# One of eight row maxima of a two-round step computed from a key-difference score, with PSUM banks and matmul order rearranged

## The chip, the cores and the metric

The kernel runs on one core of one Trainium2 chip. That core has a matrix engine (TensorE, "PE" in the profile, with its weight loads shown as "PEld"), three engines for elementwise work (VectorE "DVE", ScalarE "ACT", GpSimd "POOL") and a queue engine (SyncE "SP") that issues most DMAs. Each engine works through its own list of instructions in order and waits on semaphores for the others. Matrix products land in PSUM, which here is used as eight banks of 128 x 512 float32 each. The metric is device time in microseconds, lower is better.

## The reference

Two complete multi-head attentions (A and B) read the same input `x` of 2048 tokens x 512, each with its own `wqkv` and `wo`, 32 heads of width 16, and a per-token gate mixes their results:

```python
def mha(x, wqkv, wo):                      # S = 2048, D = 512, H = 32, Dh = 16
    q, k, v = split_heads(x @ wqkv)
    scores = einsum("bhqd,bhkd->bhqk", q, k) * Dh ** -0.5
    return merge_heads(softmax(scores) @ v) @ wo

g = sigmoid((x * gate_w).sum(-1))
out = g * mha(A_x, A_wqkv, A_wo) + (1 - g) * mha(A_x, B_wqkv, B_wo)
```

Everything is float32. The softmax needs, for each of 64 heads and 2048 queries, the maximum of 2048 scores before the exponentials, so every score is formed twice: once with queries on the partitions for the maximum, and once with keys on the partitions for the exponential and the product with the values.

## The kernel before

**Prologue.** Queries, keys and values of all heads are projected on TensorE (`project_qk`, `project_v`), split into a high and a low float32r part, and written to DRAM (`qd`, `kd`, `vd`). From there `load_stacks` brings the two operands of one head into SBUF as `q_st` and `k_st`: 48 rows (high, low and high parts of 16 features) at partitions 0 and the same again at partition 64. Two matmuls that use different halves run beside each other in the array; `rows()` hands the halves out in turn. While the last projections run, `run_ahead` already forms the maxima of the first 20 query tiles (16 of head 0, four of head 1).

**Main loop.** A round is one head and one tile of 128 keys; there are 64 x 16 = 1024 rounds, and the loop takes two at a time (`for r in range(0, ROUNDS, 2)`); these two rounds together are called a *step* below, and eight steps are a *head*. In a step TensorE does, in the order that the string `FULL` writes out:

- `e`, eight times: one score matmul (50 rows, 128 keys x 512 queries; the two extra rows subtract the maximum) into a bank of `ps_st`, whose exponential ScalarE writes to `p` (`score`).
- `m` and `M`, three parts for each of two query tiles that lie 20 tiles ahead (`max_part`): score matmuls of 128 queries x 512 keys. An `m` forms one block of 512 keys into a bank of `ps_m1` (two banks); an `M` forms two blocks into the double bank of `ps_m2`. VectorE reduces each part to its maximum, one column of `mxp`. That is four reductions over 512 and two over 1024 per step: the eight blocks of two query tiles.
- a digit: so many quarters (128 queries each) of the product of `p` with the values (`attend`), four blocks of keys side by side in the array, accumulated in the bank `acc`. A quarter's `p` was made in the step before. Before the first digit of a step the due output projections (`project_out`, 12 or 9 matmuls) are placed, in 32 steps of the run.

`tc.manual_schedule()` makes the order of the program the order on each engine. PSUM holds two banks `ps_m1`, two (one double) `ps_m2`, three `ps_st` and one `acc`; a tile of a pool takes its pool's banks in turn, and a matmul into a bank waits until the bank's previous content has been read.

**At the end of a head's maxima** (every 16 query tiles, in the steps where r mod 16 is 10), `max_split` reduces `mxp` to one value per query on VectorE (`mrow`, L135), GpSimd splits that in two (`mparts`, L136 and L137), and in the next step `max_rows` transposes it on VectorE (`mt`, L142) and sends it through DRAM into the two extra rows of `q_st`. The step with r mod 16 = 12 begins the next head's maxima. When a head's last `attend` is done (r mod 16 = 0), ScalarE copies `acc` to SBUF (`ev`, L549), and the next head's first product waits for that.

GpSimd's other work is placed by `at(round, ...)`: the gate's products (L313, L320), the value loads (L158), normalization and splitting of finished outputs (L389, L394, L395). These calls are emitted at the head of their step, ahead of the step's matmuls.

## Time and profile before

| what | value |
| --- | --- |
| median of 3 runs | 2851.66 us (2851.09 to 2851.94) |
| span of the profiled execution, first to last instruction | 2848.8 us |
| PE busy | 2830.3 us (99%) |
| DVE busy | 2559.5 us (90%) |
| ACT busy | 2260.3 us (79%) |
| POOL busy | 225.3 us (8%) |
| main loop, first exponential to the last head's maxima | about 294.6 to 2775 us |

The profiled execution's own time is its span, 2848.8 us; the runs shown have 2.9 us more. Matmuls are pipelined and their ends are modelled, so a PE that is busy 99% of the time is not for that reason at its peak. In the main loop's share of the span DVE is busy nearly all the time as well. A row of the timeline has the start in us, the length in us, the engine, the line, the operation, output and inputs, the shapes, a count where several followed each other, and in brackets the idle time before it with what ended it.

### The profile page before, as it was taken

The page shows a single profiled execution, that of the slowest core. Times are in us where ns is not written, and L with a number is a line of the kernel's source. Part 1 is how long each engine was busy: PE and PEld are TensorE (multiplying, and loading weights), DVE is VectorE, ACT ScalarE, POOL GpSimd, SP SyncE. Part 2 cuts the span into 40 slices and gives each one's busy share as a digit, 9 for nine tenths or more (in the row PEclk, how much of TensorE's full clock was granted, in tenths as well). Part 3 has the DMA queues.
Part 4 walks back from the last instruction along what each step waited for, and adds up shares of the span by engine and source line. Part 5 has one row for each costly group of instructions (what it writes and reads, how often), then busy time and mean ns, then how long its engine had stood idle before and what let it go on. Part 6 is the DMA issues. An engine that isn't in the chain of part 4 may idle for free.

```text
span 2848.8 us, 62282 instructions
## 1 busy us (share of the span) xinstructions
PE 2830.3 (99%) x26016; PEld 1372.6 (48%) x26016; DVE 2559.5 (90%) x3371; ACT 2260.3 (79%) x4253; POOL 225.3 (8%) x369
## 2 busy tenths in 40 slices
PE   8999999999999999999999999999999999999999
PEld 7877444444444444444444455444444444444544
DVE  4135899999999999999999988999999999998894
ACT  3221788889888888988988866888888888987775
POOL 1000232000000000000100231000000000011201
PEclk9999999999999999999999999999999999999999
DMA  7673333222332222332322342232222233323302
GB/s 244 195 230 121 88 80 80 40 49 54 66 58 55 52 56 46 54 56 55 85 55 49 95 101 55 54 56 48 59 47 55 55 74 66 54 67 85 72 10 91
DMA packets 83759, 214.65 MB, mean 75 GB/s; under 512 B 21878, under 2 KB 32086, under 8 KB 70934
## 3 DMA queue, kind: packets, MB, share of 16 engines
q1 hardware_dynamic: 80918, 201.76, 31.1%
q0 software_dynamic: 2560, 8.91, 1.2%
q8 instruction: 205, 3.36, 0.5%
q14 instruction: 76, 0.62, 0.1%
HBM read 145.87 MB, written 64.74 MB: 74 GB/s over the span
## 4 chain that ended last, share of the span: by engine, by line
PE 91%; DVE 7%; DMA 1%; ACT 0%; SPq 0%; issue 0%; POOL 0%; DVEq 0%; ACTq 0%
PE acc L532 34%; PE ps_st L583 29%; PE ps_m L123 14%; DVE mxp L125 7%; PE ps_pro L206 6%; PE ps_m L416 3%; PE ps_pro L229 3%; DMA raw<-in_xT 0%; DMA rb<-rd 0%; PE ps_st L416 0%; DVE rn L371 0%; PE ps_st L467 0%; ACT p L585 0%; PE ps_m L583 0%; PE ps_m L467 0%
## 5 line engine op out<-in xcount | busy, mean ns | idle before, releaser
L125 DVE TENSOR_REDUCE mxp<-ps_m 128x1 f32<-128x512 f32 (+1 forms) x3072 | 2419.6, 861 | 49.8 <-PE ps_m L123 43.5
L585 ACT ACTIVATE p<-ps_st 128x512 f32<-128x512 f32 x4056 | 2157.0, 601 | 332.6 <-PE ps_st L583 233.7
L583 PE MATMUL ps_st<-q_st,k_st 50*128 50x512 f32 x4056 | 1322.9, 445 | 0.0
L123 PE MATMUL ps_m<-k_st,q_st 48*128 48x512 f32 x4096 | 1199.0, 434 | 3.6 <-DVE mxp L125 3.1
L532 PE MATMUL acc<-p,vg 128*17 128x384 f32 (+1 forms) x16208 | 1188.3, 386 | 3.0 <-DVE ev L540 2.0
L583 PEld LDWEIGHTS ps_st<-q_st,k_st 50*128 50x128 f32 x4056 | 591.8, 184 | 745.7 <-ACT p L585 723.8
L123 PEld LDWEIGHTS ps_m<-k_st,q_st 48*128 48x128 f32 x4096 | 543.1, 185 | 105.6 <-DVE mxp L125 39.4
L532 PEld LDWEIGHTS acc<-p,vg 128*17 128x17 f32 x16208 | 314.0, 96 | 512.1 <-issue 481.0
L136 POOL CAST mparts<-mrow 128x16 fp32r<-128x16 f32 x64 | 12.5, 196 | 2194.5 <-DVE mrow L135 2194.5
L211 DVE TENSOR_TENSOR part<-ps_pro,part 128x1024 fp32r<-128x1024 f32 x32 | 39.2, 1225 | 110.5 <-ACT part L210 110.5
L210 ACT CAST part<-ps_pro 128x1024 fp32r<-128x1024 f32 x32 | 32.5, 1015 | 132.0 <-PE ps_pro L206 132.0
L416 PE MATMUL ps_m<-wo,ot 128*128 128x512 f32 (+1 forms) x354 | 90.4, 400 | 0.0
L206 PE MATMUL ps_pro<-xh,whi 128*128 128x512 f32 x256 | 73.2, 405 | 8.0 <-ACT xh L192 7.5
L232 ACT COPY v_st<-ps_pro 128x512 f32<-128x512 f32 x31 | 18.2, 587 | 77.4 <-PE ps_pro L229 77.4
L416 PEld LDWEIGHTS ps_m<-wo,ot 128*128 128x128 f32 (+1 forms) x354 | 64.0, 188 | 23.8 <-DVE mxp L125 8.7
L206 PE MATMUL ps_pro<-xh,wlo 128*128 128x512 f32 x256 | 69.3, 393 | 0.0
L206 PE MATMUL ps_pro<-xl,whi 128*128 128x512 f32 x256 | 69.2, 393 | 0.0
L206 PEld LDWEIGHTS ps_pro<-xh,whi 128*128 128x128 f32 x256 | 47.9, 192 | 23.1 <-ACT xh L192 10.2
L206 PEld LDWEIGHTS ps_pro<-xh,wlo 128*128 128x128 f32 x256 | 48.6, 190 | 10.3
L206 PEld LDWEIGHTS ps_pro<-xl,whi 128*128 128x128 f32 x256 | 48.6, 190 | 10.2
L180 DVE TENSOR_TENSOR wlo<-wraw,whi 128x512 fp32r<-128x512 f32 x16 | 10.9, 684 | 46.8 <-ACT whi L179 46.8
L549 ACT COPY ev<-acc 128x512 f32<-128x512 f32 x63 | 38.2, 607 | 0.0
(92 smaller groups left out, 634.4 us busy)
## 6 DMA issues: line engine op xcount, KB each, us to landing
k_st<-kd SPq DMA_DIRECT2D x128, 256.0 KB
q_st<-qd SPq DMA_DIRECT2D x128, 256.0 KB
qd<-part SPq DMA_DIRECT2D x32, 512.0 KB
kd<-part SPq DMA_DIRECT2D x32, 512.0 KB
k_st<-kd SPq DMA_DIRECT2D x128, 128.0 KB
q_st<-qd SPq DMA_DIRECT2D x128, 128.0 KB
od<-ev SPq DMA_DIRECT2D x63, 256.0 KB
vd<-v_st SPq DMA_DIRECT2D x32, 272.0 KB
```

Of the source, the lines that this page charges most:

```text
L123: pe.matmul(ps[:, i * 512:(i + 1) * 512], q[b:b + SC, t * P:(t + 1) * P], k[b:b + SC, c * 512:(c + 1) * 512], start=True, stop=True)
L125: dve.tensor_reduce(mxp[h][:, t, part:part + 1], ps, op=ALU.max, axis=AX.X)
L206: pe.matmul(ps[:, c * 512:(c + 1) * 512], a[:, k], b[:, k], start=n == 0, stop=n == 3 * KC - 1)
L210: act.copy(pt[0], ps)
L211: dve.tensor_tensor(pt[1], ps, pt[0].bitcast(F32), op=ALU.subtract)
L229: pe.matmul(ps[:, :DM], a[:, k, o:o + P], b[:, k], start=n == 0, stop=n == 3 * KC - 1)
L232: act.copy(v_st[t % 2][:, :, 0:16], v)
L416: pe.matmul(ps, ot[a][:n, slot, sl], wt[b][:n, g], start=G == groups[0] and i == 0, stop=G == groups[-1] and i == 2)
L532: pe.matmul(acc[32 * c:32 * c + 17, qa * P:qb * P], v[:, 4 * a + c if final else kt, j], p[:, c * 512 + qa * P:c * 512 + qb * P], start=fi ...
L549: act.copy(ev, acc)
L583: pe.matmul(ps, k[b:b + SC + 2, kk * P:(kk + 1) * P], q[b:b + SC + 2, cc * 512:(cc + 1) * 512], start=True, stop=True)
L585: act.activation(pt[r][:, c * 512:(c + 1) * 512], ps, AF.Exp, scale=SCALE)
```

## The change

Of the eight blocks of 512 keys whose maximum a step forms, two are now taken in one VectorE operation. For the first query tile of the step, blocks 0 and 1 are combined by max(s0, s1) = s1 + max(s0 - s1, 0):

- A fifth block of 512 columns is added to the keys in DRAM and to `k_st` (`KS` = 2560): the difference of keys 0 to 511 and keys 512 to 1023. `key_difference` computes it on GpSimd in the prologue, five operations for each of the eight key projections, and two more DMAs write it. `load_stacks` loads 2560 columns of keys in place of 2048.
- `max_excess` (`r` in `FULL`) forms the score of the difference into a bank of `ps_st`, and ScalarE writes its positive part to SBUF (`excess`).
- `max_pair` (`f`) forms the score of block 1 into a bank of `ps_m`; VectorE adds `excess` and reduces to the maximum (`tensor_tensor_reduce`, built as two instructions: the operation over 512 and a read-out of one column).
- Six blocks remain as single reductions over 512. A step then has eight score matmuls for maxima as before, seven operations over 512 on VectorE, and nine on ScalarE.
- `mxp` gets four columns per query tile; the column that is not written is preset by a GpSimd `memset` of the whole tile at the start of each head's maxima.
- PSUM: `ps_m1` and `ps_m2` become one pool `ps_m` of three banks, `ps_st` gets four. The prologue's `run_ahead` forms four single blocks per query tile through the three banks.
- `FULL` becomes `mree2emem3ememef3me`, the digits 2, 3, 3 in place of 3, 2, 3. In the last rounds scores take three of seven banks from `ps_m`. The last head's split results are put into free parts of `q_st` and `k_st`.

```diff
+LOWEST = -3.0e38
+KS = S + 512
...
-    ps_m1 = ctx.enter_context(tc.tile_pool(name="ps_m1", bufs=2, space=PSUM))
-    ps_m2 = ctx.enter_context(tc.tile_pool(name="ps_m2", bufs=1, space=PSUM))
+    ps_m = ctx.enter_context(tc.tile_pool(name="ps_m", bufs=3, space=PSUM))
...
-            dma(k[b:b + 32].bitcast(F32), pairs(ks, HG * DH * S))
+            dma(k[b:b + 32].bitcast(F32), pairs(ks, HG * DH * KS, KS))
...
         turn[0] ^= 1
         return HALVES[1 - turn[0]]
+    def max_tile(m):
+        h, t = divmod(m, NT)
+        if t == 0 and h not in mxp:
+            mxp[h] = small.tile([P, NT, NQ], F32, name="mxp")
+            if h:
+                pool.memset(mxp[h], LOWEST)
+        return h, t
+
+    def max_scores(ps, h, t, c):
+        q, k = q_st[h % 3], k_st[h % 3]
+        b = rows()
+        pe.matmul(ps, q[b:b + SC, t * P:(t + 1) * P], k[b:b + SC, c * 512:(c + 1) * 512], start=True, stop=True)
+
     def max_part(m, part):
+        h, t = max_tile(m)
+        ps = ps_m.tile([P, 512], F32, name="ps_m")
+        max_scores(ps, h, t, part)
+        dve.tensor_reduce(mxp[h][:, t, part:part + 1], ps, op=ALU.max, axis=AX.X)
+
+    excess = {}
+
+    def max_excess(m):
+        h, t = max_tile(m)
+        ps = ps_st.tile([P, 512], F32, name="ps_st")
+        max_scores(ps, h, t, NQ)
+        excess[m] = work.tile([P, 512], F32, name="excess")
+        act.activation(excess[m], ps, AF.Relu)
+
+    def max_pair(m):
         h, t = divmod(m, NT)
-        if t == 0 and part == 0:
-            mxp[h] = small.tile([P, NT, 3], F32, name="mxp")
-        q, k = q_st[h % 3], k_st[h % 3]
-        chunks = PARTS[part]
-        n = len(chunks)
-        ps = (ps_m1 if n == 1 else ps_m2).tile([P, n * 512], F32, name=f"ps_m{n}")
-        for i, c in enumerate(chunks):
-            b = rows()
-            pe.matmul(ps[:, i * 512:(i + 1) * 512], q[b:b + SC, t * P:(t + 1) * P],
-                      k[b:b + SC, c * 512:(c + 1) * 512], start=True, stop=True)
-        dve.tensor_reduce(mxp[h][:, t, part:part + 1], ps, op=ALU.max, axis=AX.X)
-
-
+        ps = ps_m.tile([P, 512], F32, name="ps_m")
+        max_scores(ps, h, t, 1)
+        e = excess.pop(m)
+        dve.tensor_tensor_reduce(e, ps, e, 1.0, LOWEST, ALU.add, ALU.max, mxp[h][:, t, 1:2])
     mparts = {}
...
+
+        def key_difference(dst, parts):
+            d = [pro.tile([P, 512], F32, name=f"kdiff{i}", bufs=1) for i in range(2)]
+            for i in range(2):
+                pool.tensor_tensor(d[i], parts[i][:, :512], parts[i][:, 512:], op=ALU.subtract)
+            pool.tensor_tensor(d[0], d[0], d[1], op=ALU.add)
+            hi = pro.tile([P, 512], F32R, name="kdiff_hi", bufs=1)
+            lo = pro.tile([P, 512], F32R, name="kdiff_lo", bufs=1)
+            pool.tensor_copy(hi, d[0])
+            pool.tensor_tensor(lo, d[0], hi.bitcast(F32), op=ALU.subtract)
+            for i, t in enumerate((hi, lo)):
+                nc.sync.dma_start(dst[i].rearrange("h d t -> (h d) t")[:, S:], t.bitcast(F32))
...
+                if isk and half == 0:
+                    key_difference(dst, [t.bitcast(F32) for t in pt])
...
-        ahead = [(m, part) for m in range(NT + LEAD) for part in range(3)]
+        ahead = [(m, part) for m in range(NT + LEAD) for part in range(NQ)]
...
-            project_qk(s, g, isk, lambda: run_ahead((i >= 10) + (i >= 13)))
+            project_qk(s, g, isk, lambda: run_ahead((i >= 10) + 2 * (i >= 13)))
...
-                run_ahead(3)
+                run_ahead(4)
-    ps_st = ctx.enter_context(tc.tile_pool(name="ps_st", bufs=3, space=PSUM))
+    ps_st = ctx.enter_context(tc.tile_pool(name="ps_st", bufs=4, space=PSUM))
...
     def score_bank(r):
         if r >= ROUNDS - NT - LEAD:
             late[0] += 1
-            if late[0] % 6 in (1, 3):
-                return ps_m1.tile([P, 512], F32, name="ps_m1")
-            if late[0] % 6 == 5:
-                return ps_m2.tile([P, 1024], F32, name="ps_m2")[:, :512]
+            if late[0] % 7 in (1, 3, 5):
+                return ps_m.tile([P, 512], F32, name="ps_m")
         return ps_st.tile([P, 512], F32, name="ps_st")
     def score(r, c):
...
-    FULL = "e3eemm2eMeme3emeM"
+    FULL = "mree2emem3ememef3me"
...
             load_stacks(h + 2)
         m = r + NT + LEAD
-        scored = parts = 0
+        scored, parts = 0, 2
         for step in FULL if m < ROUNDS else ():
             if step == "e":
                 score(r + scored // 4, scored % 4)
                 scored += 1
-            elif step in "mM":
-                max_part(m + parts // 3, parts % 3)
+            elif step == "r":
+                max_excess(m)
+            elif step == "f":
+                max_pair(m)
+            elif step == "m":
+                max_part(m + parts // NQ, parts % NQ)
                 parts += 1
             else:
                 for a in projects:
```

How the change moves instructions is shown at three places. First TensorE in the main loop, from the long product (`acc`, 17 x 384 columns, four side by side) that ends one step. In the rows before, L583 is the score for the exponential, L123 a score for a maximum, L532 the product with the values; a step reads:

```order
L532 MATMUL acc<-p,vg 17x384 x4
L583 MATMUL ps_st<-q_st_117,k_st_118 128x512 x2
L123 MATMUL ps_m_15263<-k_st_2011,q_st_2010 128x512
L123 MATMUL ps_m_15266<-k_st_2011,q_st_2010 128x512
L532 MATMUL acc<-p,vg 17x128 x8
L583 MATMUL ps_st<-q_st_117,k_st_118 128x512
L123 MATMUL ps_m_15280<-k_st_2011,q_st_2010 128x512 x2
L583 MATMUL ps_st<-q_st_117,k_st_118 128x512
L123 MATMUL ps_m_15288<-k_st_2011,q_st_2010 128x512
L583 MATMUL ps_st<-q_st_117,k_st_118 128x512
L532 MATMUL acc<-p,vg 17x384 x4
```

In the changed kernel the same place reads as follows; L614 is the score for the exponential, L124 a score for a maximum (the one into `ps_st` is the key difference), L565 the product:

```order
L565 MATMUL acc<-p,vg 17x384 x4
L124 MATMUL ps_m<-k_st_2137,q_st_2136 128x512
L614 MATMUL ps_st<-q_st_114,k_st_115 128x512
L124 MATMUL ps_m<-k_st_2137,q_st_2136 128x512
L124 MATMUL ps_st<-k_st_2137,q_st_2136 128x512
L614 MATMUL ps_st<-q_st_114,k_st_115 128x512 x2
L565 MATMUL acc<-p,vg 17x256 x4
L614 MATMUL ps_st<-q_st_114,k_st_115 128x512
L124 MATMUL ps_m<-k_st_2137,q_st_2136 128x512
L614 MATMUL ps_st<-q_st_114,k_st_115 128x512
L124 MATMUL ps_m<-k_st_2137,q_st_2136 128x512
L565 MATMUL acc<-p,vg 17x256 x4
```

The rows of the change go on with `L565` over 128 columns, six matmuls (scores and maxima in turn) and the long product. Both steps have groups of six, four and six matmuls between three products, and every group fills the two halves of the array in pairs; what changes is where the two kinds stand in a group, and that the products cover 256, 256 + 128 and 384 columns where they covered 384, 128 + 128 and 384.

Second, VectorE where one head's maxima end and the next head's begin, with what each row waits for. Before (L125 is a maximum, L135 `mrow`, L142 the transpose):

```order
L125 TENSOR_REDUCE mxp<-ps_m_11338 128x1 [waits PE_49]
L135 TENSOR_REDUCE mrow<-mxp 128x16 [waits DVE_49]
L125 TENSOR_REDUCE mxp<-ps_m_11362 128x1 [waits PE_49]
L125 TENSOR_REDUCE mxp<-ps_m_11365 128x1 [waits PE_49]
L142 STREAM_TRANSPOSE mt<-mparts 128x32 [waits DMAHW6_49,Pool_49]
```

In the changed kernel (L130 is a maximum, L146 the combined one in its two instructions, L154 `mrow`, L161 the transpose):

```order
L146 ISA excess,mxp<-ps_m,excess 128x512 [waits PE_49,Activation_49]
L146 ISA mxp 128x1
L130 TENSOR_REDUCE mxp<-ps_m 128x1 [waits PE_49]
L154 TENSOR_REDUCE mrow<-mxp 128x16 [waits DVE_49]
L130 TENSOR_REDUCE mxp<-ps_m 128x1 [waits PE_49,Pool_49]
L161 STREAM_TRANSPOSE mt<-mparts 128x32 [waits DMAHW4_49]
L130 TENSOR_REDUCE mxp<-ps_m 128x1 [waits PE_49] x4
```

The first maximum of the new head, which waited for TensorE alone, now waits for GpSimd too. On GpSimd, what it waits for stands behind the two operations on `mrow`, and in some steps behind other work; two ends of heads in a row of the changed kernel read:

```order
L155 CAST mparts<-mrow 128x16 [waits DVE_49]
L156 TENSOR_TENSOR mparts<-mrow,mparts 128x16 [waits Pool_49]
L118 MEMSET mxp 128x64
L155 CAST mparts<-mrow 128x16 [waits DVE_49]
L156 TENSOR_TENSOR mparts<-mrow,mparts 128x16 [waits Pool_49]
L422 TENSOR_TENSOR o_num<-o_num,rb 128x512 [waits DMAHW1_49,DMAHW0_49]
L422 TENSOR_TENSOR o_num<-o_num,rb 128x512 [waits DMAHW3_49,DMAHW2_49]
L118 MEMSET mxp 128x64
```

The `memset` did not exist before; it is now the last of the three or more operations that follow `mrow` on GpSimd.

Third, TensorE in the prologue, between two projections of values (L229 before, L262 after). Before, each bundle of maxima uses two single banks and the double one:

```order
L229 MATMUL ps_pro<-wvlo,xh_133 128x512 x4
L123 MATMUL ps_m_1681<-k_st_114,q_st_113 128x512
L123 MATMUL ps_m_1684<-k_st_114,q_st_113 128x512
L123 MATMUL ps_m_1687<-k_st_114,q_st_113 128x512 x2
L229 MATMUL ps_pro<-wvhi,xh_134 128x512 x4
```

In the changed kernel:

```order
L262 MATMUL ps_pro<-wvlo,xh_131 128x512 x4
L124 MATMUL ps_m<-k_st_111,q_st_110 128x512 x4
L262 MATMUL ps_pro<-wvhi,xh_131 128x512 x4
L262 MATMUL ps_pro<-wvhi,xl_135 128x512 x4
L262 MATMUL ps_pro<-wvlo,xh_131 128x512 x4
```

The four matmuls stand where they stood; they now take four tiles from a pool of three banks.

## The prediction, made before the run

> **What bounds the kernel now.** I read the page's busy times first, then the windows over the main loop, the groups by shape, and one step of the timeline.

> ```profile
> PE 2830.3 (99%) x26016; PEld 1372.6 (48%) x26016; DVE 2559.5 (90%) x3371; ACT 2260.3 (79%) x4253; POOL 225.3 (8%) x369
> ```
> ```profile
> 1000.00:1500.00 500.00, 499.81 (x5046) 220.98 (x5042) 498.40 (x659) 449.09 (x855) 18.88 (x42) 1.00 0.30 57
> ```
> ```profile
> L125 DVE TENSOR_REDUCE mxp<-ps_m 128x1 f32<-128x512 f32 x2048 | 1313.1, 683 | 43.6 <-PE ps_m L123 43.5
> L125 DVE TENSOR_REDUCE mxp<-ps_m 128x1 f32<-128x1024 f32 x1024 | 1246.3, 1217 | 6.2 <-PE ps_st L583 0.8
> ```

> In the window of 500 us (columns PE, PEld, DVE, ACT, POOL) PE and DVE are both full, ACT has 10% left. Which of the two full ones sets the pace shows in the timeline of PE: one step, from one long product to the third product after it.

> ```profile
> 1505.67 0.84 PE L532 MATMUL acc<-p,vg 128*17 128x384 f32 x8
> ...
> 1506.44 0.50 PE L583 MATMUL ps_st<-q_st,k_st 50*128 50x512 f32 x2
> ...
> 1507.09 0.63 PE L532 MATMUL acc<-p,vg 128*17 128x128 f32 x16
> ...
> 1507.65 0.49 PE L583 MATMUL ps_st<-q_st,k_st 50*128 50x512 f32 x1
> ...
> 1508.00 0.39 PE L583 MATMUL ps_st<-q_st,k_st 50*128 50x512 f32 x1
> ...
> 1508.23 0.39 PE L583 MATMUL ps_st<-q_st,k_st 50*128 50x512 f32 x1
> ...
> 1508.54 0.84 PE L532 MATMUL acc<-p,vg 128*17 128x384 f32 x8
> ...
> 1509.31 0.50 PE L583 MATMUL ps_st<-q_st,k_st 50*128 50x512 f32 x1
> ...
> 1510.36 0.84 PE L532 MATMUL acc<-p,vg 128*17 128x384 f32 x8
> ```

> The step takes 1510.36 - 1505.67 = 4.69 us: product 0.77, group of four 0.65, short products 0.56, group of six 0.89, product 0.77, group of six 1.05. The two groups of six hold the same work, so the second waits 0.16: PE alone would need 4.53. VectorE needs all of it. Two reductions of 512 behind each other start 0.60 apart (below: 1.28 for two, the last 0.68), so operations overlap by 0.08, one of 1024 costs 1.217 - 0.08 = 1.13, and 4 x 0.60 + 2 x 1.13 = 4.66. **VectorE sets the pace by 0.13 us per step; TensorE is right behind it.**

> Over eight steps the pace includes what happens at a head's end. GpSimd's rows on `mrow` mark it:

> ```profile
> 367.42 0.20 POOL L136 CAST mparts<-mrow 128x16 fp32r<-128x16 f32 x1 [7.65 <-DVE mrow L135]
> ...
> 367.88 1.29 POOL L313 TENSOR_TENSOR num<-num,gate_b 128x512 f32<-128x512 f32 x1
> ...
> 405.46 0.20 POOL L136 CAST mparts<-mrow 128x16 fp32r<-128x16 f32 x1 [7.65 <-DVE mrow L135]
> ...
> 443.50 0.20 POOL L136 CAST mparts<-mrow 128x16 fp32r<-128x16 f32 x1 [7.11 <-DVE mrow L135]
> ```

> A head takes 38.04 us, 0.5 more than eight steps.

> **The change part by part.** *VectorE's work.* It loses two reductions of 1024 (2.27) and gains two of 512 (1.20) and the combined operation with its read-out, T. No row shows T; the nearest are

> ```profile
> L211 DVE TENSOR_TENSOR part<-ps_pro,part 128x1024 fp32r<-128x1024 f32 x32 | 39.2, 1225 | 110.5 <-ACT part L210 110.5
> L422 DVE SCALAR_TENSOR_TENSOR o_acc<-ps_m,gate,o_acc 128x512 f32<-128x512 f32 x22 | 16.5, 751 | 11.2 <-PE ps_m L416 11.2
> ```
> ```profile
> 1587.58 1.21 DVE L125 TENSOR_REDUCE mxp<-ps_m 128x1 f32<-128x1024 f32 x1
> 1588.83 0.20 DVE L135 TENSOR_REDUCE mrow<-mxp 128x16 f32<-128x48 f32 x1
> 1588.95 1.28 DVE L125 TENSOR_REDUCE mxp<-ps_m 128x1 f32<-128x512 f32 x2
> 1590.14 0.20 DVE L142 STREAM_TRANSPOSE mt<-mparts 128x32 f32<-128x32 f32 x1
> ```

> A second operand beside one in PSUM costs nothing there (1225 against 1217 over 1024), a small operation 0.12 from start to start (1588.83 to 1588.95). So T is at least 0.60, at most 0.75 + 0.20 = 0.95 with nothing overlapped; I take 0.60 + 0.12 = 0.73, nearest to the L211 row. VectorE then needs 6 x 0.60 + 0.73 = 4.33 per step.

> *ScalarE* gets a ninth operation:

> ```profile
> 1500.49 1.57 ACT L585 ACTIVATE p<-ps_st 128x512 f32<-128x512 f32 x3
> ...
> 1506.97 4.45 ACT L585 ACTIVATE p<-ps_st 128x512 f32<-128x512 f32 x8 [0.22 <-PE ps_st L583]
> ```

> Eight fill 4.45 because they wait for scores; undisturbed, three take 1.57, so (1.57 - 0.60) / 2 = 0.485 apart, and nine need 4.37. [...]

> *TensorE* keeps sixteen matmuls in groups of six, four and six, and 1024 product columns. The 256 columns that now stand alone I take as 0.55 (near the 0.56 of two times 128; ends 0.38, half the long one, and 0.57). 0.89 + 0.55 + 0.65 + 0.77 + 0.89 + 0.77 = 4.52; with the rounding of the stamps I take 4.53. This is the longest of the three, so the step should become **4.53, TensorE's**. With starts at 0, 0.34, 0.57 | 1.44, 1.78 | 2.86, 3.20, 3.43 for the pairs of a step, every bank of both pools comes free in time: the tightest is the combined maximum's at 3.43, which needs the bank three maxima earlier, read until about 3.35.

> *The end of a head.* New is the wait of the next head's first maximum for GpSimd's `memset`, which stands behind the two operations on `mrow`:

> ```profile
> 1589.10 0.20 POOL L136 CAST mparts<-mrow 128x16 fp32r<-128x16 f32 x1 [37.94 <-DVE mrow L135]
> 1589.37 0.22 POOL L137 TENSOR_TENSOR mparts<-mrow,mparts 128x16 fp32r<-128x16 f32 x1
> 1589.55 3.76 POOL L389 TENSOR_TENSOR o_num<-o_num,rb 128x512 f32<-128x512 f32 x3
> ```
> ```profile
> L219 POOL MEMSET v_st<- 128x32 f32 x2 | 0.2, 160 | 0.1
> L158 POOL DMA_DIRECT2D vg<-vd x32 | 24.5, 767 | 138.2 <-DMA vd<-v_st 136.0 <-PE ps_st L583 1.2 <-PE ps_m L123 0.7
> L371 DVE RECIPROCAL rn<-dn 128x64 f32<-128x64 f32 x14 | 7.6, 543 | 0.0
> ```

> From `mrow` (1588.83) GpSimd's third operation begins 0.72 later; with 0.19 for 64 columns (0.16 for 32) and 0.07 for the signal (1589.03 to 1589.10) VectorE goes on after 0.98 in place of 0.12. Behind it queue the transpose and all later maxima. In TensorE's clock of the step: the last maximum of the old head starts at 0.79, `mrow` at 1.51 (0.68 and 0.04 later), the new head's first at 2.49, transpose, then the next at 3.22 and 3.82. The combined maximum's bank is the last one's: read at 4.50, free at 4.57, wanted at 3.43. TensorE stands still for **1.13** and, being the bound, doesn't make it up. VectorE's spare time of 0.2 per step is no help, since three banks hold no more than that. Below zero it cannot be; above, GpSimd's other work adds to it one to one: the gate's product (1.28) in four heads, a value load (0.79) in six, normalizations (two of 1.29) in two of the plain heads and the split of the last weights (about 1.9) in one: 5.1 + 4.7 + 5.2 + 1.9 = 16.9.

> *ScalarE's copy of `acc`*, hidden under VectorE so far, now counts:

> ```profile
> PEld acc L532 <- ACT ev L549: 23.6, 63, 1.2
> PEld ps_m L416 <- DVE mxp L125: 8.7, 24, 0.4
> ```

> 23.6 / 63 = 0.37 is the upper end, nothing the lower; queued behind nine operations it ends some 0.15 late for the product and delays the fifth score by 0.06 more: I take 0.25 per head.

> *Steps with output projections* (32) are TensorE's already; the wait of 0.36 for a bank shrinks (8.7 / 24): -0.14 each, -4.5. In six of them the late `memset` plus two normalizations reach the bank after the projection: 1.4 each, +8.

> *The two halves of a reciprocal* (L371, 14 in all) no longer set the pace: -5.

> *Prologue.* Four single tiles come from three banks, fourteen times:

> ```profile
> 252.29 0.73 PE L123 MATMUL ps_m<-k_st,q_st 48*128 48x512 f32 x4
> ...
> 252.82 2.42 DVE L125 TENSOR_REDUCE mxp<-ps_m 128x1 f32<-128x512 f32 x3 [1.16 <-PE ps_m L123]
> 252.95 1.18 PE L229 MATMUL ps_pro<-wvhi,xh 128*128 128x512 f32 x4
> ```

> The fourth must wait for the first reduction: 252.82 + 0.68 + 0.07 = 253.57, where it started 0.34 after 252.29. TensorE, busy throughout that stretch, loses 0.94 x 14 = **13.2**. The key differences on GpSimd, 4.2 MB of DMA and the longer loads lie beside idle queues; I cost them at nothing (a late load would hold a head's first maxima).

> **The sum.** Of 502 steps 470 are plain, 58.75 heads' worth; 62 heads have the new wait, 54 of them in plain steps.

> - steps: (8 x 4.53 - 38.04) x 58.75 = -1.80 x 58.75 = -105.8
> - copies of `acc`: 0.25 x 58.75 = +14.7
> - waits for the `memset`: 1.13 x 54 = +61.0, other GpSimd work +16.9
> - projections -4.5 + 8 = +3.5; reciprocals -5
> - prologue +13.2

> Together -1.5: 2848.8 - 1.5 = 2847.3 for the profiled execution, and with the 2.9 by which the median of the runs lies above it about **2850**. A difference up to 0.2% (5.7 us) is about what a measurement of this kernel can't tell from no change, so the forecast is no change worth naming: what the shorter step gives is handed back at the heads' ends and in the prologue.

> **The rivals.** *The combined operation is slow and VectorE stays the bound* (slower). A head is then 8 x (3.60 + T) + 0.36 + 0.88, which passes TensorE's 37.6 at T = 0.95. At T = 1.0 a head is as long as now and nothing pays for the rest: 16.9 + 3.5 + 13.2 - 0.88 x 4.75 = +29, 2881. For it: two instructions, a kind the trace doesn't show. Against: the L211 row. [...]

> *The head's end stays hidden* (faster): if VectorE didn't wait, or PSUM had more slack than I count, 61 + 17 disappear: 2772. For it: VectorE has 0.2 spare per step. Against: its row names GpSimd's semaphore, and GpSimd works in order.

> *ScalarE and its four banks hold the step* (slower): 4.37 of 4.53 leaves 0.16, and the second score of the pair at 0.57 needs a bank read 0.02 earlier. A step of 4.61 costs 0.08 x 470 = +38: 2888.

> **How the numbers follow.** The forecast has a chance of 0.53, with 2830 to 2868 as its own range (step +-0.02: 9 us; the wait 0.9 to 1.4: 15; copies 0 to 0.37: 15), of it 0.24 faster, 0.16 the same, 0.13 slower. Slow combined operation 0.18 (0.17 slower, 0.01 the same), hidden end 0.17 (faster), ScalarE 0.12 (0.09 slower, 0.03 the same). Faster 0.41, same 0.20, slower 0.39. 2795 to 2900 leaves out most of the hidden end and the part of the slow operation above T = 1.05, about 0.2.

> **What would show it.** Right: DVE busy clearly below its 498 of 500 in a window, steps of 4.53 whose groups of six take 0.89 both; between `mrow` and the next maximum a gap near 1 us put down to GpSimd, and TensorE waiting on VectorE once per head; in the prologue a bundle of four at 1.6 in place of 0.66. Wrong: T above 0.95, ScalarE without idle time, or no gap behind `mrow`.

## The result, and the profile after

The changed kernel takes 2902.14 us (median, 2899.51 to 2908.22), the kernel before 2851.8 beside it: a ratio of 1.0179, with a 95% interval of 1.0164 to 1.0193. It is 1.8% slower. The forecast was 2850 with a range of 2795 to 2900, so both the value and the range were wrong. The profiled execution took 2899.51 us; its span is 2897.7, 48.9 longer than before.

The busy times of the page, and then the window of 500 us in the middle of the loop (columns PE, PEld, DVE, ACT, POOL, granted clock, DMA share, GB/s):

```profile
PE 2851.4 (98%) x26016; PEld 1437.6 (50%) x26016; DVE 2396.4 (83%) x4395; ACT 2420.3 (84%) x4755; POOL 280.0 (10%) x472
```
```profile
1000.00:1500.00 500.00, 497.71 (x4994) 231.75 (x4996) 460.61 (x862) 476.68 (x950) 20.23 (x55) 0.99 0.34 63
```

VectorE is no longer full (460.6, where it had 498.4), ScalarE nearly is (476.7, where it had 449.1), and TensorE has gaps. What the change was made of did happen: the combined operation is cheap. The timeline of VectorE, around a head's end and around one combined operation:

```profile
1505.76 0.22 DVE L154 TENSOR_REDUCE mrow<-mxp 128x16 f32<-128x64 f32 x1
1506.66 0.69 DVE L130 TENSOR_REDUCE mxp<-ps_m 128x1 f32<-128x512 f32 x1 [0.69 <-POOL mxp L118]
...
1514.57 0.68 DVE L146 CUSTOM_DVE_ANT_0 excess<-ps_m,excess 128x512 f32<-128x512 f32 x1
1515.18 0.08 DVE L146 DVE_READ_ACCUMULATOR2_ANT mxp<- 128x1 f32 x1
1515.18 1.28 DVE L130 TENSOR_REDUCE mxp<-ps_m 128x1 f32<-128x512 f32 x2
```

From the combined operation to the next reduction it is 1515.18 - 1514.57 = 0.61, the same as for one plain reduction, and the read-out starts together with that reduction. The wait at the head's end is there too: 0.90 from `mrow` to the next maximum, put down to GpSimd's `memset`.

One plain step in the timeline of TensorE, from one long product to the next of its kind:

```profile
1513.70 0.84 PE L565 MATMUL acc<-p,vg 128*17 128x384 f32 x8
1514.47 0.49 PE L124 MATMUL ps_m<-k_st,q_st 48*128 48x512 f32 x1
...
1515.05 0.48 PE L614 MATMUL ps_st<-q_st,k_st 50*128 50x512 f32 x2
1515.46 0.63 PE L565 MATMUL acc<-p,vg 128*17 128x256 f32 x8
1516.02 0.50 PE L614 MATMUL ps_st<-q_st,k_st 50*128 50x512 f32 x1
...
1516.68 0.84 PE L565 MATMUL acc<-p,vg 128*17 128x256 f32 x16
1517.45 0.50 PE L614 MATMUL ps_st<-q_st,k_st 50*128 50x512 f32 x1
...
1518.36 0.84 PE L565 MATMUL acc<-p,vg 128*17 128x384 f32 x8
```

This step is 4.66 and not 4.53. Of the two groups of six, one (1517.45 to 1518.36) takes 0.91, the other (1514.47 to 1515.46, the end `me` of the order and its start `mree`) 0.99. Over the trace the medians are 0.90 and 0.97, and undisturbed steps (those not at a head's end and without the copy of `acc`) last 4.58 to 4.65, 4.62 on average.

GpSimd's rows on `mrow` mark the heads again:

```profile
1506.04 0.20 POOL L155 CAST mparts<-mrow 128x16 fp32r<-128x16 f32 x1 [37.49 <-DVE mrow L154]
...
1506.48 0.15 POOL L118 MEMSET mxp<- 128x64 f32 x1
1544.14 0.20 POOL L155 CAST mparts<-mrow 128x16 fp32r<-128x16 f32 x1 [37.51 <-DVE mrow L154]
```

A plain head (one without the gate's work, loads or output projections) takes 38.10 us, where it took 38.04: the shorter step is given back in full at its end. So the 48.9 us don't come from the plain heads at all. With these marks the whole execution can be divided (in us; the last two columns are experiments told of below):

| stage | before | after | E1 | E5 |
| --- | --- | --- | --- | --- |
| to the mark of the second head | 329.4 | 343.6 | 345.2 | 331.2 |
| 5 heads with the gate's work on GpSimd | 191.2 | 204.4 | 187.8 | 187.8 |
| 5 heads with a load of values or weights | 190.3 | 197.8 | 187.1 | 187.1 |
| 10 heads with output projections | 462.1 | 479.6 | 456.0 | 456.2 |
| 42 plain heads | 1603.0 | 1600.7 | 1574.1 | 1574.3 |
| after the last mark | 72.7 | 71.6 | 72.8 | 72.0 |

The prologue loses 14, the twenty heads in which GpSimd or the projections have more to do lose 38. Something else is in those heads, which the prediction did not have. In the first of these heads, windows of 5 us (columns as above, the granted clock third from the end), and the timeline of TensorE just before:

```profile
385.00:390.00 5.00, 3.96 (x37) 1.51 (x34) 3.04 (x9) 4.22 (x9) 3.45 (x8) 0.99 0.02 5
390.00:395.00 5.00, 5.00 (x25) 1.73 (x27) 2.87 (x6) 2.48 (x5) 0.99 (x1) 0.50 0.24 63
395.00:400.00 5.00, 5.00 (x48) 1.87 (x46) 3.78 (x8) 3.49 (x7) 1.99 (x5) 0.83 0.17 33
```
```profile
388.55 0.49 PE L124 MATMUL ps_m<-k_st,q_st 48*128 48x512 f32 x1 [0.75 <-DVE mxp L130]
...
389.24 0.50 PE L124 MATMUL ps_m<-k_st,q_st 48*128 48x512 f32 x1 [0.20 <-DVE mxp L130]
...
390.53 1.48 PE L565 MATMUL acc<-p,vg 128*17 128x384 f32 x8
```

TensorE stands still for about 1 us in the window 385 to 390, and from 389.9 on its clock is halved for 6.8 us: the long product takes 1.48 in place of 0.84. The mean clocks of the two kernels, before and after, sum that up:

```profile
core 0: 2848.8 us, clock 0.998
```
```profile
core 0: 2897.7 us, clock 0.992
```

0.2% of 2848.8 is 6 us of clock lost, 0.8% of 2897.7 is 23; the trace's list of clock changes gives 5.1 and 23.9 within the work. **Up to 18.8 us of the 48.9 are a slower TensorE**, in stretches that follow stalls at heads' ends (up to, since TensorE may also wait while its clock is halved).

### The profile page after: what moved, and what is told of

It is laid out like the page before. It is cut to its first block, busy times and chain, and to the rows that moved or that the text cites. A ratio compares the mean times of both kernels' runs of the same rounds, so it can differ in the third digit from the quotient of the medians.

```text
span 2897.7 us, 65030 instructions
## 1 busy us (share of the span) xinstructions
PE 2851.4 (98%) x26016; PEld 1437.6 (50%) x26016; DVE 2396.4 (83%) x4395; ACT 2420.3 (84%) x4755; POOL 280.0 (10%) x472
## 3 DMA queue, kind: packets, MB, share of 16 engines
q0 software_dynamic: 2560, 8.91, 1.2%
## 4 chain that ended last, share of the span: by engine, by line
PE 83%; DVE 11%; DMA 2%; POOL 2%; issue 1%; SPq 1%; ACT 0%; POOLq 0%; ACTq 0%; DVEq 0%
PE acc L565 33%; PE ps_st L614 26%; PE ps_m L124 13%; DVE mxp L130 8%; PE ps_pro L237 5%; PE ps_pro L262 3%; PE ps_m L449 2%; DVE excess L146 1%; PE ps_st L124 1%; DMA raw<-in_xT 0%; DMA qd<-part 0%; DVE mrow L154 0%; POOL o_num L422 0%; POOL mparts L155 0%; POOL mparts L156 0%
## 5 line engine op out<-in xcount | busy, mean ns | idle before, releaser
L130 DVE TENSOR_REDUCE mxp<-ps_m 128x1 f32<-128x512 f32 x3092 | 1984.6, 684 | 251.6 <-PE ps_m L124 97.6
L614 PE MATMUL ps_st<-q_st,k_st 50*128 50x512 f32 x4061 | 1377.5, 442 | 0.3 <-ACT excess L139 0.3
L124 PE MATMUL ps_m<-k_st,q_st 48*128 48x512 f32 x3594 | 1304.2, 448 | 30.1 <-DVE mxp L130 24.5
L565 PE MATMUL acc<-p,vg 128*17 128x256 f32 (+2 forms) x16208 | 1195.4, 388 | 2.6 <-DVE ev L573 1.6
L614 PEld LDWEIGHTS ps_st<-q_st,k_st 50*128 50x128 f32 x4061 | 677.2, 185 | 380.9 <-ACT p L616 219.8
L124 PEld LDWEIGHTS ps_m<-k_st,q_st 48*128 48x128 f32 x3594 | 611.7, 185 | 441.4 <-DVE mxp L130 402.0
L565 PEld LDWEIGHTS acc<-p,vg 128*17 128x17 f32 x16208 | 323.6, 96 | 536.8 <-issue 412.8
L146 DVE CUSTOM_DVE_ANT_0 excess<-ps_m,excess 128x512 f32<-128x512 f32 x502 | 341.7, 681 | 0.0
L139 ACT ACTIVATE excess<-ps_st 128x512 f32<-128x512 f32 x502 | 300.9, 599 | 1.9 <-POOL k_st L81 1.8
L124 PE MATMUL ps_st<-k_st,q_st 48*128 48x512 f32 x502 | 206.3, 411 | 0.0
L242 DVE TENSOR_TENSOR part<-ps_pro,part 128x1024 fp32r<-128x1024 f32 x32 | 39.2, 1224 | 110.9 <-ACT part L241 91.9
L124 PEld LDWEIGHTS ps_st<-k_st,q_st 48*128 48x128 f32 x502 | 92.9, 185 | 0.2 <-issue 0.2
L237 PEld LDWEIGHTS ps_pro<-xh,whi 128*128 128x128 f32 x256 | 47.9, 191 | 23.6 <-ACT xh L211 10.2
```

The source lines that it names most:

```text
L124: pe.matmul(ps, q[b:b + SC, t * P:(t + 1) * P], k[b:b + SC, c * 512:(c + 1) * 512], start=True, stop=True)
L130: dve.tensor_reduce(mxp[h][:, t, part:part + 1], ps, op=ALU.max, axis=AX.X)
L139: act.activation(excess[m], ps, AF.Relu)
L146: dve.tensor_tensor_reduce(e, ps, e, 1.0, LOWEST, ALU.add, ALU.max, mxp[h][:, t, 1:2])
L237: pe.matmul(ps[:, c * 512:(c + 1) * 512], a[:, k], b[:, k], start=n == 0, stop=n == 3 * KC - 1)
L242: dve.tensor_tensor(pt[1], ps, pt[0].bitcast(F32), op=ALU.subtract)
```

## The experiments

Three theories had to be told apart from their rivals: that GpSimd's `memset` is what the heads' ends wait for, that ScalarE's ninth operation lengthens the step, and that three banks lengthen the prologue. A fourth came with the trace: that a stall of TensorE costs more than its own length.

**E1: no `memset` between heads.** Four tiles for `mxp` are kept and preset once; from the third head on two of them alternate, and their unwritten columns stay as they were.

```diff
+    mxk = [const.tile([P, NT, NQ], F32, name=f"mxk{i}") for i in range(4)]
+    for t in mxk[1:]:
+        pool.memset(t, LOWEST)
...
-            mxp[h] = small.tile([P, NT, NQ], F32, name="mxp")
-            if h:
-                pool.memset(mxp[h], LOWEST)
+            mxp[h] = mxk[h if h < 2 else 2 + h % 2]
```

> The changed kernel, but mxp lives in four tiles that are kept for good and preset once in the prologue, so that no memset stands between two heads' maxima. Theory (the wait for GpSimd's memset costs TensorE 0.84 us in every plain head, GpSimd's other work ahead of it comes on top one to one, and the idle time also sets off the halved-clock stretches): a plain head falls from 38.10 to 37.2, the heads of the gate and of the projections lose their 2 to 8 us of excess, the halved clock falls from 24.4 us lost to under 10, and the time from 2902 to 2815 to 2830. Rival (the head's end is bound by VectorE's own mrow and transpose, or ScalarE takes over at once): plain heads stay above 37.8 and the time above 2875.

Measured: 2823.22 us, 0.9902 of the kernel before (0.9887 to 0.9917). The heads' marks, the clock and the window:

```profile
1507.08 0.20 POOL L156 CAST mparts<-mrow 128x16 fp32r<-128x16 f32 x1 [36.91 <-DVE mrow L155]
...
1544.57 0.20 POOL L156 CAST mparts<-mrow 128x16 fp32r<-128x16 f32 x1 [36.99 <-DVE mrow L155]
```
```profile
core 0: 2823.0 us, clock 0.998
```
```profile
1000.00:1500.00 500.00, 500.00 (x5135) 237.99 (x5132) 473.15 (x884) 489.04 (x976) 18.92 (x42) 1.00 0.34 63
```

79 us less than the changed kernel (74.7 by the spans), by a preset that isn't repeated. A plain head takes 37.4 to 37.5, TensorE has no gap left, and the clock is back at 0.998. By the table, 51 us of the gain come from the twenty special heads and 27 from the 42 plain ones. One detail missed: the plain head falls by 0.68, not by 0.9. The step at the head's end goes from 5.46 to 4.77, so 0.69 of it was the wait, and 0.15, with 0.08 in the step before, stays; I put that down to VectorE's own `mrow` and transpose, which I had counted into the wait.

**E2: no positive part on ScalarE.**

```diff
-        excess[m] = work.tile([P, 512], F32, name="excess")
-        act.activation(excess[m], ps, AF.Relu)
...
-        e = excess.pop(m)
-        dve.tensor_tensor_reduce(e, ps, e, 1.0, LOWEST, ALU.add, ALU.max, mxp[h][:, t, 1:2])
+        dve.tensor_reduce(mxp[h][:, t, 1:2], ps, op=ALU.max, axis=AX.X)
```

> The changed kernel without ScalarE's positive part: the matmul of the key difference stays, its bank is read by nobody, and block 1 is reduced alone (block 0 is left out of the maxima of the first query tile). TensorE's and GpSimd's work and the number of VectorE's operations are unchanged, ScalarE has eight operations per step in place of nine. Theory (ScalarE and its four banks hold the group mree plus me at 0.97 in place of 0.89): that group falls to 0.89, steps from 4.62 to 4.55, the time by 0.07 x 470 = 33 to about 2869. Rival (two score matmuls paired with each other, or the ninth matmul, cost the 0.08 by themselves): group and time unchanged, 2895 to 2905.

Measured: 2878.67 us, 1.0098 (1.0083 to 1.0113), 23.5 less than the changed kernel. The group `me` and `mree` in TensorE's timeline now reads

```profile
707.68 0.50 PE L124 MATMUL ps_m<-k_st,q_st 48*128 48x512 f32 x1
...
708.26 0.41 PE L611 MATMUL ps_st<-q_st,k_st 50*128 50x512 f32 x2
708.60 0.63 PE L562 MATMUL acc<-p,vg 128*17 128x256 f32 x8
```

0.92 in place of 0.99; its median over 468 groups falls from 0.971 to 0.917, the undisturbed step from 4.62 to 4.577, and the step in which ScalarE copies `acc` from 4.83 to 4.63. The plain head falls from 38.10 to 37.66. So ScalarE's ninth operation does hold TensorE, although all nine fit into the step. How, TensorE's weight loads of the two groups show, of the changed kernel and then of E2:

```profile
1514.82 0.39 PEld L614 LDWEIGHTS ps_st<-q_st,k_st 50*128 50x128 f32 x2
```
```profile
708.03 0.32 PEld L611 LDWEIGHTS ps_st<-q_st,k_st 50*128 50x128 f32 x2
```

Two loads of 0.18 fill 0.39, so the second begins at 1515.03, 0.56 after the start of its group; without the ninth operation it is 0.49 (708.17 after 707.68). What these loads wait for stands in the table of waits, here from 550 to 850 us, again of the changed kernel and of E2 (total, times, longest):

```profile
PEld ps_st L614 <- ACT p L616: 29.2, 77, 0.4
```
```profile
PEld ps_st L611 <- ACT p L613: 10.3, 49, 0.2
```

These loads wait until ScalarE has read the bank that their matmul will write. Over the trace the group follows that load: of 409 undisturbed groups of the changed kernel, the 60 whose last load begins about 0.35 after the start take 0.90, the 176 at about 0.49 take 0.92, the 173 at about 0.56 take 0.98, and the profile puts every load of the last two kinds down to ScalarE's exponential. The recorded start of the second matmul, 1515.05, hardly moves with it; that it runs late is inferred from the product behind it.

E2 also drops VectorE's read-out and its wait for `excess`; that every late load waits for ScalarE speaks against these as the cause. The ninth operation costs 0.044 in each step and 0.15 in each copy. Over 470 steps and 62 copies that makes 30 us; the total shows 23.5, in part because E2 loses 4 us more to a halved clock (27.9 against 23.9). The other 0.047 by which the step lies above 4.53 stays without it. Most is my own rounding (0.557, 0.663 and 0.902 where I had 0.55, 0.65 and 0.89). The rest is this group's 0.917 in place of 0.902: with eight operations, too, its last load waits for ScalarE in 351 of 415 groups.

**E3: a fourth bank for the prologue's maxima.** A pool of one bank, open during the prologue, takes every fourth maximum.

```diff
+            tc.tile_pool(name="ps_x", bufs=1, space=PSUM) as ps_x:
...
-        ps = ps_m.tile([P, 512], F32, name="ps_m")
+        if spare and len(spare) % 4 == 0:
+            ps = ps_x.tile([P, 512], F32, name="ps_x")
+        else:
+            ps = ps_m.tile([P, 512], F32, name="ps_m")
```

> The changed kernel, but in the prologue every fourth maximum takes a bank of its own (a fourth bank, given back before the main loop). Theory (the fourth matmul of each bundle waits for the bundle's first reduction, 1.71 in place of 0.66, thirteen times): bundles go back to 0.66, the main loop starts 13 us earlier, time about 2888. Rival (VectorE needs 2.48 for four reductions and holds the next bundle, or the late start is due to the third stack's memset): less than 5 us.

Measured: 2887.11 us, 1.0129 (1.0112 to 1.0146), 15 less (11.8 by the spans). TensorE's timeline in the prologue, of the changed kernel and then of E3:

```profile
261.29 0.73 PE L124 MATMUL ps_m<-k_st,q_st 48*128 48x512 f32 x3
262.57 0.49 PE L124 MATMUL ps_m<-k_st,q_st 48*128 48x512 f32 x1 [0.55 <-DVE mxp L130]
262.99 1.20 PE L262 MATMUL ps_pro<-wvhi,xh 128*128 128x512 f32 x4
```
```profile
248.52 0.73 PE L124 MATMUL ps_m<-k_st,q_st 48*128 48x512 f32 x3
248.87 0.39 PE L124 MATMUL ps_x<-k_st,q_st 48*128 48x512 f32 x1
249.19 1.20 PE L270 MATMUL ps_pro<-wvhi,xh 128*128 128x512 f32 x4
```

The bundle (the four maxima between two projections) goes from 1.70 to 0.67. The mark of the second head comes at 331.8, where the changed kernel has 343.6 and the kernel before 329.4: the third bank was 12 of the 14 us that the prologue lost, and the other 2 were not traced.

**E4: eight single reductions in the new pools and order.**

```diff
-            if h:
-                pool.memset(mxp[h], LOWEST)
...
-    FULL = "mree2emem3ememef3me"
+    FULL = "mmee2emem3ememem3me"
...
-        scored, parts = 0, 2
+        scored, parts = 0, 0
```

> The new pools, prologue and matmul order alone: no key-difference score, all eight blocks reduced one by one through the three banks, ScalarE with eight operations, no memset at the heads. Theory (VectorE sets the pace when it has to do eight reductions): step 8 x 0.60 = 4.80 to 4.85, head about 38.9, time 2851.7 + 0.85 x 58.75 + 14 for the prologue = 2905 to 2925, VectorE full. Rival (TensorE or ScalarE hold the step at 4.6 whatever VectorE does): 2815 to 2840, since no head's end waits for GpSimd.

Measured: 3072.14 us, 1.0775 (1.0759 to 1.0791). Neither theory had that. The plain head is 41.3, the step 5.16. The window, and TensorE's timeline of the group behind a long product:

```profile
1000.00:1500.00 500.00, 491.62 (x4645) 216.29 (x4641) 483.92 (x802) 424.19 (x786) 13.94 (x35) 1.00 0.30 57
```
```profile
1024.02 0.50 PE L122 MATMUL ps_m<-k_st,q_st 48*128 48x512 f32 x1
...
1024.36 1.00 PE L122 MATMUL ps_m<-k_st,q_st 48*128 48x512 f32 x2
1024.87 0.72 PE L612 MATMUL ps_st<-q_st,k_st 50*128 50x512 f32 x2
1025.52 0.63 PE L563 MATMUL acc<-p,vg 128*17 128x256 f32 x8
```

That group takes 1.50 where it had 0.97. In this order three maxima stand in the group before it and three in it, and with three banks the later ones have to wait for VectorE's reductions of the earlier ones. The weight load of the group's third maximum does:

```profile
1024.87 0.18 PEld L122 LDWEIGHTS ps_m<-k_st,q_st 48*128 48x128 f32 x1 [0.41 <-DVE mxp L128]
```

VectorE, whose eight need 4.8 of the 5.16, lacks work elsewhere in the step. E8 asks whether this is the cause.

**E8: eight single reductions, spread.** As E4 with E3's bank and `FULL = "mmeeme3meme2mmeeem3"`.

> Eight single reductions again, no key-difference score and no memset, with the prologue's fourth bank and an order that spreads the maxima 3, 2 and 3 over the groups and has the digits 3, 2, 3 (mmeeme3meme2mmeeem3). Theory (what made eight singles in the first order slow was six maxima in two neighbouring groups over three banks, a step of 5.16 of which VectorE was busy 4.5; spread out, its eight reductions of 0.60 and the hand-over of three banks set the step): step 4.85 to 5.0, head 39.2 to 40.4, time 2915 to 2985. Rival (eight maxima through three banks cost 5.16 in any order): head 41.3, time 3050 to 3065.

Measured: 2948.44 us, 1.0347 (1.033 to 1.0364), step 4.90, head 39.4, and VectorE is full:

```profile
1000.00:1500.00 500.00, 499.91 (x4866) 217.53 (x4862) 499.55 (x839) 444.31 (x825) 18.91 (x42) 1.00 0.33 62
```

It is 124 us less than E4, of which E3's bank gives 12 to 15; the rest comes from the order. So the burst was the cause in E4, and spread out, VectorE's eight reductions set the pace. Against E5, which has the combined operation, the ninth operation on ScalarE and another order, 138 us lie between them. How much of that is the combined operation and how much the order, no run separates.

**E5: E1 and E3 together.**

> The two mendings together: the kept, once preset mxp and the prologue's fourth bank for maxima. Theory (they act in different stages and add up): 2823 - 15 = 2808, which is 1.5% below the kernel before; plain heads 37.4, halved clock under 8 us lost. Rival (the earlier start is lost again at the first heads, where the two meet): 2815 to 2823.

Measured: **2810.48 us, 0.9859 (0.9842 to 0.9875) of the kernel before.** That is 2.5 us from the sum of the two, and the version beats both kernels. In the window TensorE has no gap left:

```profile
1000.00:1500.00 500.00, 500.00 (x5132) 237.44 (x5128) 473.24 (x886) 488.87 (x976) 19.35 (x44) 1.00 0.33 63
```

ScalarE, with 488.9 of 500, is the engine next to full.

**E6: a longer wait.**

```diff
-                pool.memset(mxp[h], LOWEST)
+                for _ in range(10):
+                    pool.memset(mxp[h], LOWEST)
```

> The changed kernel with ten memsets of mxp in place of one at each head, which makes VectorE's wait 0.9 to 1.3 us longer per head (0.10 to 0.15 each) and changes nothing else. Theory (a stall costs its length, and beyond that the clock is halved for about 6.8 us, 3.4 lost, when TensorE idles for more than about 1 us within one of the 3.41-us stretches in which the recorded clock changes): the recorded clock loss rises from 24 us to 100 to 200, heads come in two kinds, 39.1 and about 42.5, and the time is 3040 to 3130. Rival (the wait costs only its own length, and the halved clock in the gate's heads has another cause): all plain heads near 39.2, clock loss unchanged, time 2955 to 2980.

Measured: 3191.53 us, 1.1198 (1.1181 to 1.1214). GpSimd's row, the wait's row and the clock:

```profile
1044.22 2.03 POOL L119 MEMSET mxp<- 128x64 f32 x10
```
```profile
DVE mxp L131 <- POOL mxp L119: 190.3, 63, 6.8
```
```profile
core 0: 3187.9 us, clock 0.923
```

The ten take 2.03, so the wait grew by 1.88 a head and not by the 0.9 to 1.3 expected: 117 us over 62 heads. The time grew by 289. The clock lost is 7.7% of 3187.9, 245 us, 222 more than in the changed kernel (their sum, 339, is not reached; part of the halved clock presumably falls where TensorE waits anyway). A plain head is 42.9 in the median, 4.8 more for 1.88 of wait. That the heads come in two kinds was too simple: the halved stretches are 3.4, 6.8, 10.2 and once 13.7 long, and nearly every head has one. The rival, a wait that costs its length, would have given some 3020 with the wait's true size; it is out.

**E7: E5 with the copy of `acc` on VectorE.**

```diff
-            act.copy(ev, acc)
+            dve.tensor_copy(ev, acc)
```

> As the two mendings together, with the copy of acc at each head's end on VectorE in place of ScalarE. Theory (the step with the copy takes 4.83 in place of about 4.62 because the copy queues behind ScalarE's nine operations, and VectorE has 0.3 to spare per step): that step falls to about 4.65, 0.18 x 63 = 11 us less than the two mendings alone. Rival (the copy holds up VectorE's maxima by 0.6 in a step that has three banks): the step stays at 4.8 or grows, no gain or a loss of up to 20 us.

Measured: 2826.97 us, 0.9918 (0.9903 to 0.9932), 16.5 more than E5. The step with the copy takes 5.11 in place of 4.83. The three steps behind it gain only 0.07 together. VectorE and the waiting product in E7, and the copy on ScalarE in E5:

```profile
1475.72 0.68 DVE L153 CUSTOM_DVE_ANT_0 excess<-ps_m,excess 128x512 f32<-128x512 f32 x1
...
1476.33 0.69 DVE L592 COPY ev<-acc 128x512 f32<-128x512 f32 x1
```
```profile
1477.07 0.63 PE L575 MATMUL acc<-p,vg 128*17 128x256 f32 x8 [0.47 <-DVE ev L592]
```
```profile
1468.39 0.61 ACT L592 COPY ev<-acc 128x512 f32<-128x512 f32 x1
```

The copy begins 0.71 after the start of the group in front of the product (1475.62), because it stands behind the combined operation; on ScalarE it was 0.30 (after 1468.09). The product comes 0.49 later, and the group of four behind it gives 0.20 back. The rival had the time right, but not the way: it is the product that the copy holds up, not the maxima.

## Why the prediction was wrong

Its sum, term by term, against the profiled execution (us; the measured terms are worked out as the predicted ones, from the undisturbed step of 4.62, the copy's step at 0.21 and the head's end at 0.84 + 0.08 above it; halved clock is the whole loss by the list of clock changes; the row above the sum is what remains of 48.9):

| term | predicted | measured |
| --- | --- | --- |
| steps, 58.75 x (8 x step - 38.04) | -105.8 | -63.5 |
| copies of `acc`, 58.75 x | +14.7 | +12.3 |
| wait at the head's end, 54 x | +61.0 | +49.7 |
| prologue | +13.2 | +14.3 |
| halved clock | none | +18.8 |
| GpSimd's other work, projections, reciprocals, tail | +15.4 | +17.3 |
| sum | -1.5 | +48.9 |

**The step that failed first** is the one on TensorE: "This is the longest of the three, so the step should become 4.53, TensorE's", resting on "every bank of both pools comes free in time". The mechanism (VectorE no longer sets the pace) was right, the size was off by 0.09: a step of 4.62, which times 470 steps is 42 us. E2 gives 0.044 of it to ScalarE's ninth operation. I had compared ScalarE's sum, 4.37, with the step, found room, and asked of each bank only when the matmul wants it. But the weights are loaded ahead of the matmul (in that group, from 1514.71 for the one at 1514.80), and the last score's load begins 0.56 after the start of the group, where E2 has 0.49: the condition is earlier than the one I tested. My third rival had the place, the banks and the number, "A step of 4.61", and got 0.12. It deserved more, since the prediction itself put that margin at 0.02, while it called another bank, with 0.08 to spare, the tightest.

ScalarE's own pace was not the error: undisturbed, seven exponentials take 3.56 in the changed kernel's trace, which is (3.56 - 0.60) / 6 = 0.49 apart, where I had taken 0.485.

```profile
1516.00 3.56 ACT L616 ACTIVATE p<-ps_st 128x512 f32<-128x512 f32 x7
```

**The second** is a term that was not in the sum. I priced each stall of TensorE at its own length. In the heads where GpSimd had more in front of the `memset` TensorE stood still for longer, and behind six of these stalls (0.6 to 3.9 us) the clock was halved; E1 removes stall and halving together, E6 makes both larger. The wait itself was taken 11 us too large, which hid part of the two errors in the total.

What held: *T* came out at 0.61 (0.73 taken, 0.60 the lower bound), which puts an end to the rival of a slow combined operation. The wait for the `memset` is where it was put, 0.90 against 0.98 after `mrow`, and E1 shows that it costs TensorE 0.69 in a plain head; with VectorE's own two operations the head's end is 0.92 against 1.13. GpSimd's other work in front of it adds to it, as said. The prologue was right in place and size (bundles of 1.70 against 1.6; 14.3 against 13.2), and E3 takes 12 of the 14 away. The copies were right in size; E2 shows that 0.15 of their 0.21 come from the ninth operation. The rival with a hidden head's end was wrong in its condition, but its price can now be compared: 2772 without wait, and E1, which takes the wait away, has 2823. The 51 us between them are for the most part the longer step (42) and VectorE's own share of the head's end (0.23 x 54 = 12).

Of the observations that were to decide, "steps of 4.53 whose groups of six take 0.89 both" failed at once, and ScalarE "without idle time" was nearly seen (476.7 of 500, 489.0 in E1). The range was too narrow above: it ended at 2900 because the cases were added one at a time, and a longer step beside a longer head's end was in none of them.

## What to carry to other kernels

Before an engine is called the new bound, walk through the hand-over of every bank with the time that the weights need ahead of the matmul (0.18 us a load here): ScalarE at 95% of the time (476.7 of 500) already cost 0.044 us per step here. Look for constants that are set again in a loop behind other work on their engine; keeping the preset tiles was worth 79 us. And do not price a stall of TensorE at its length alone: in E6, 117 us more of waiting cost 289, because a halved clock followed (0.923 in the mean, where the changed kernel has 0.992).

## What the runs showed of the hardware

The other one is the two-instruction reduction: its read-out of one column starts together with the next reduction and adds nothing to the 0.61 us from the operation's start to the next.
